# Gate and up projections in pairs of 64-row TensorE tiles, in a fused attention and gated-MLP kernel

## The chip, the cores and the metric

The kernel is one program on one core of a Trainium2 chip. A core has TensorE (PE, matrix products, with its weight loads shown apart as PEld), VectorE (DVE), ScalarE (ACT), GpSimd (POOL) and SyncE (SP, which issues most DMAs). The metric is the device time of the program in microseconds (us); lower is better. The three timed runs shown of the kernel before took 615.78, 615.84 and 615.91 us, median 615.84. The profiled execution took 615.51 us; its span, from the first to the last instruction of the program, is 613.8 us, so 1.7 us lie around the span. The granted TensorE clock was 1.00 over the whole span.

## The reference, cut to what matters

```
xn  = layernorm(x)                         # x: 2048 x 576, no gain or bias
qkv = xn @ wqkv                            # 32 heads of 18
s   = q @ k.T * 18**-0.5                   # query i sees keys i-255 .. i
o   = softmax(s) @ v
h   = silu(xn @ w1) * (xn @ w3)            # 4608 wide: gate w1, up w3
out = x + o @ wo + h @ w2
```

All operands are bf16. Both branches start from the same normalised `xn`, and both end in one sum.

## The kernel before

**Chunks and stages.** The 2048 rows are worked in four chunks of 512 (`c` = 0 to 3). Each chunk has two stages. Stage 1 makes gate, up and `h` for 36 units `u` of 128 hidden columns, and between the units the attention scores, their exps and the products with V. Stage 2 multiplies `h` by `w2` and the attention output by `wo` into four PSUM banks, one for each block of 128 rows, in two passes of 288 columns; beside it the Q, K and V of the next chunk are projected. A prologue normalises chunk 0 and projects its Q, K and V.

**Order.** All engines' work is written out by hand with `add(engine, ...)` in one order. Each engine runs its own instructions in that order, and semaphore waits come from the buffers that an instruction reads and writes. So an instruction that waits holds up all that stands behind it on its engine.

**A unit.** The contraction is 576 deep, which is four blocks of 128 and a rest of 64. `unit_full` (L551, matmuls L556) does the four whole blocks for up and for gate: eight matmuls of 128 x 512, over all 128 rows of the array. `unit_rest` (L561, L567) does the rest in tiles of 32 rows: two for up and two for gate, on two of the array's four row groups. If the unit has an attention step, `window_scores` (L572) puts that step's scores (L460) on the other two row groups. A head is 18 deep and sits in a group of 32 rows. Units without a step are worked in pairs (`window_pair`, L584): both units' rests share the four row groups. There are 120 step units and 12 such pairs.

**A step.** A step is one block of 128 keys for four heads, `g` being the group of heads and `s` the step's number (1 to 3 in chunk 0, else 0 to 3). Its scores are 384 columns a head, one PSUM bank for each head. In steps 0 and 3 a head's columns come from two matmuls. `exps` (L473) runs twice for two heads each, and `masks` (L485) makes four triangle cuts on POOL. Two units after the last step of a group, `pv` (L504) multiplies by V in tiles of 32 array columns, DVE copies the sums to `uT` (L513), `heads_back` (L520) transposes them with four 128 x 128 matmuls, and `heads_out` (L527, L529) divides and stores.

**h.** `us = up * 0.5` (DVE, L593), `th = tanh(gate / 2)` (ACT, L599), `gs = (th + 1) * gate` (DVE, L605), `h = gs * us` (DVE, L608).

**The next chunk's input.** In stage 1 DVE also normalises the next chunk's four blocks of rows: statistics L320 to L322, apply L334 (four instructions, since the 64-row rest is stored four times in two orders for the 32-row tiles). PE transposes a block with six matmuls (L343) and DVE copies it out (L347).

**PSUM.** Four banks go round as a ring for gate, up, `pv` and the transposes; the other four hold the scores in stage 1 and the sums of stage 2.

**Weights.** `load_w13` (L284) brings 512 columns of `w3` and of `w1` at a time into three buffers, and `load_wr` (L296) the 64-row rests apart. `repack` (L413) moves Q and K from `stage` into the layout of the scores by DMA: on SP in chunk 0, on ACT later.

The two lines on which the order inside a step unit rests:

```
unit_rest(c, u, 0); heads 0 and 1; first part of heads 2 and 3
unit_rest(c, u, 1); what is left of heads 2 and 3
```

Of the kernel before, what the change touches and what calls it, by code (L numbers as in the profile page):

```python
# [5 lines left out]
dt = mybir.dt  # L6
# [7 lines left out]
class _Op:  # L14
    __slots__ = ("eng", "fn", "deps", "pos", "sig", "dma", "cnt", "snap", "waits")

    def __init__(self, eng, fn, deps, dma):
        self.eng = eng
        self.fn = fn
        self.deps = deps  # L20
        self.dma = dma
        self.pos = 0
        self.sig = False
        self.cnt = 0
        self.snap = None
        self.waits = ()

# [16 lines left out]
class _Prog:  # L44
# [13 lines left out]
    def add(self, eng, fn, r=(), w=(), j=(), dma=None):  # L58
# [11 lines left out]
        op = _Op(eng, fn, deps, dma)  # L70
# [17 lines left out]
    def resolve(self):  # L88
        know = {e: {} for e in ENGS}
        for op in self.ops:  # L90
            kn = know[op.eng]
            need = {}
            for d in op.deps:
                if d.dma is not None:
                    s, v = ("d", d.dma), d.cnt
                else:
                    if d.eng == op.eng and (d.eng == "pe" or d.eng == "sp"):
                        continue
                    s, v = d.eng, d.pos
# [63 lines left out]
def bass_parallel_sum__sliding_block__glu_gated_swiglu__prompt_kernel(  # L163
# [32 lines left out]
    with ExitStack() as es:  # L196
# [4 lines left out]
        NXP, NOF, NPT, NW13, NW2 = 7, 4, 14, 3, 4  # L201
        ident = sb("ident", [128, 128])
        xp = [sb(f"xp{i}", [128, D]) for i in range(NXP)]
        xn = [sb(f"xn{i}", [128, 768]) for i in range(2)]
# [5 lines left out]
        xnT = sb("xnT", [128, 2, 6, CH])  # L210
        wa = sb("wa", [128, 5, 3 * D])
        wo = sb("wo", [128, 5, D])
        w1 = [sb(f"w1_{i}", [128, 4, 512]) for i in range(NW13)]
        w3 = [sb(f"w3_{i}", [128, 4, 512]) for i in range(NW13)]
        wr = sb("wr", [128, 2, F // 2])
# [3 lines left out]
        qk = sb("qk", [128, 3, G, CH])  # L219
        va = sb("va", [128, 2 * TB, G, 4 * VW])  # L220
        pt = sb("pt", [128, NPT, 2, 384])
        NST = 9 * CH // 768
        pt_more = stage[:, :, :].rearrange("p t c -> p (t c)").rearrange("p (n h q) -> p n h q", h=2, q=384)
# [7 lines left out]
        def st_keys(*tiles):  # L231
            return [("sh", 2 * t + n) for t in tiles for n in range(2)]
# [6 lines left out]
        us = [sb(f"us{i}", [128, CH]) for i in range(2)]  # L239
# [4 lines left out]
        RB = es.enter_context(nc.psum_tensor("rb", [128, 4, 512], dt.float32))  # L244
        SBK = es.enter_context(nc.psum_tensor("sbk", [128, 4, 512], dt.float32))
# [9 lines left out]
        def half_bank(b):  # L255
            return RB[:, b, :].bitcast(dt.bfloat16)

# [18 lines left out]
        def load_w13():  # L276
# [6 lines left out]
            for n, (dst, src) in enumerate(((w3, B_w3), (w1, B_w1))):  # L283
                add("sp", lambda e, dst=dst, src=src: e.dma_start(  # L284
                    dst[s][:], src[0:512, c0:c0 + 512].rearrange("(kd p) f -> p kd f", p=128)),
                    dma=f"w13_{s}", **{"j" if n else "w": [("w13", s)]})

        WR_CUTS = (0, 4, 10, F // 256)

        def load_wr(n):  # L290

            n0, n1 = WR_CUTS[n:n + 2]
            for q in range(4):
                src = (B_w3, B_w1)[q % 2][512:576, :].rearrange("(ab p) (n u f) -> p ab n u f", p=32, u=2, f=128)
                for ab in range(2):
                    add("sp", lambda e, q=q, ab=ab, src=src: e.dma_start(  # L296
                        wr[32 * q:32 * q + 32, ab, n0 * 128:n1 * 128].rearrange("p (n f) -> p n f", f=128),
                        src[:, ab, n0:n1, q // 2, :]),
                        dma=f"wr{n}", **{"j" if q or ab else "w": [("wr", n)]})

        def wr_key(u):
            return ("wr", max(n for n in range(3) if WR_CUTS[n] <= u // 2))

# [14 lines left out]
        def ln_stats(t, s):  # L318
            i = t % 2
            add("dve", lambda e: e.bn_stats(stats[i][:, 0, :], xp[s][:, 0:HD]), r=[("xp", s)], w=[("stats", i)])  # L320
# [7 lines left out]
        def ln_apply(t, s):  # L328
            i = t % 2
            tail = xn[i][:, 512:768].rearrange("p (m a r d) -> p m a r d", m=2, r=2, d=32)  # L330
            xtail = xp[s][:, 512:576].rearrange("p (a d) -> p a d", d=32).unsqueeze(2).to_broadcast([128, 2, 2, 32])
            moves = ((xn[i][:, 0:512], xp[s][:, 0:512]), (tail[:, 0], xtail), (tail[:, 1, 0], xtail[:, 1]), (tail[:, 1, 1], xtail[:, 0]))
            for n, (dst, src) in enumerate(moves):
                add("dve", lambda e, dst=dst, src=src: e.tensor_scalar(  # L334
                    dst, src, mv[i][:, 0:1], rstd[i][:, 0:1], op0=ALU.subtract, op1=ALU.mult),
                    r=[("xp", s), ("mv", i), ("rstd", i)], **{"j" if n else "w": [("xn", i)]})

        def xn_trans(t, bank, key, evac):
            i = t % 2
            c, tt = divmod(t, TB)  # L340
            bv = bank.rearrange("p (k f) -> p k f", f=128)
            for kd in range(6):
                add("pe", lambda e, kd=kd: e.transpose(bv[:, kd, :], xn[i][:, kd * 128:(kd + 1) * 128], ident[:]),  # L343
                    r=[("xn", i), "ident"], **{"w" if kd == 0 else "j": [key]})
            dst = xnT[:, c % 2, :, tt * 128:(tt + 1) * 128]
            if evac == "dve":
                add("dve", lambda e: e.tensor_copy(dst, bv[:, 0:6, :]), r=[key], w=[("xnT", c % 2, tt)])  # L347
            else:
                add("act", lambda e: e.activation(dst, bv[:, 0:6, :], ACT.Copy), r=[key], w=[("xnT", c % 2, tt)])
# [5 lines left out]
        def qk_tile(c, i):  # L355
            b = ring()
            for kd in range(5):
                add("pe", lambda e, kd=kd: e.matmul(  # L358
                    RB[:, b, :], wa[:, kd, i * 128:(i + 1) * 128], xnT[:, c % 2, kd, :],
                    start=(kd == 0), stop=(kd == 4)),  # L360
                    r=["wqk", "wz"] + xk(c), **{"w" if kd == 0 else "j": [("rb", b)]})
            add("dve", lambda e: e.tensor_copy(stage[:, i, :], RB[:, b, :]), r=[("rb", b)], w=st_keys(i))  # L362

        def v_half(c, tt, half, evac):
# [3 lines left out]
            for kd in range(5):  # L368
                add("pe", lambda e, kd=kd: e.matmul(  # L369
                    RB[:, b, 0:HD], xnT[:, c % 2, kd, tt * 128:(tt + 1) * 128], wa[:, kd, c0:c0 + HD],  # L370
                    start=(kd == 0), stop=(kd == 4)),
                    r=["wv", "wz", ("xnT", c % 2, tt)], **{"w" if kd == 0 else "j": [("rb", b)]})
            vv = va[:, slot, :, :].rearrange("p g (hh c) -> p (g hh) c", c=VW)
            dst = vv[:, 16 * half:16 * half + 16, 0:Dh]
            src = RB[:, b, 0:HD].rearrange("p (h d) -> p h d", d=Dh)
            kw = {"w" if half == 0 else "j": [("va", slot)]}
            if evac == "act":
                add("act", lambda e: e.activation(dst, src, ACT.Copy), r=[("rb", b)], **kw)
            else:
                add("dve", lambda e: e.tensor_copy(dst, src), r=[("rb", b)], **kw)  # L380
# [16 lines left out]
        def repack(c, g, eng):  # L397
# [4 lines left out]
            for hh in range(4):  # L402
                b = 1 + c % 2
                for tq, tk, rq, rk, o, n in pieces(Dh * (4 * g + hh)):
                    p0 = 64 * (g % 2) + 32 * (hh % 2) + o
                    gi = 2 * (g // 2) + hh // 2
                    if tq != tk:
                        moves = [(qk[p0:p0 + n, 0:b + 1:b, gi, :], stage[rq:rq + n, tq:tk + 1:tk - tq, :])]
                    else:
                        moves = [(qk[p0:p0 + n, 0, gi, :], stage[rq:rq + n, tq, :]),  # L410
                                 (qk[p0:p0 + n, b, gi, :], stage[rk:rk + n, tk, :])]
# [41 lines left out]
        def score_mms(c, g, s, h):  # L453

            r0 = 64 * (g % 2) + 32 * (h % 2)
            gi = 2 * (g // 2) + h // 2
            for n, (kb, qb, nq, col) in enumerate(parts(c, s)):
                kc, kt = divmod(kb, TB)
                qo = (qb - c * TB) * 128
                add("pe", lambda e, kc=kc, kt=kt, qo=qo, nq=nq, col=col: e.matmul(  # L460
                    SBK[:, h, col:col + 128 * nq],
                    qk[r0:r0 + Dh, 1 + kc % 2, gi, kt * 128:(kt + 1) * 128],
# [386 lines left out]
```

## Time and profile before

| what | value |
|---|---|
| median of the timed runs | 615.84 us |
| profiled execution / its span | 615.51 / 613.8 us |
| busy share PE, DVE, ACT, POOL | 97%, 64%, 43%, 36% |
| prologue | 0 to 25.53 us |
| chunk 0: stage 1, stage 2 | 94.04, 57.34 us |
| chunk 1: stage 1, stage 2 | 92.46, 57.49 us |
| chunk 2: stage 1, stage 2 | 92.47, 57.50 us |
| chunk 3: stage 1, stage 2 | 91.07, 45.89 us |
| DMA | 75.42 MB, mean 123 GB/s |

A stage 1 is counted from its first weight load of L556 to the first of L640, a stage 2 from there to the next stage 1 or the end. The profile names an instruction group by line, engine and tiles. A matmul's duration in the profile (0.38 us for 128 x 512) contains the way through the array; what a following matmul must wait for is the distance between two starts, which is 0.2157 us for matmuls of 128 x 512 one behind the other. Starts are given here to the nanosecond where the trace has them.

### The profile page before, as it was taken

The numbers are of one execution on the slowest core, as the hardware profiler recorded it, in microseconds if no ns is written. First come the engines' busy times: TensorE is split into PE (matmuls) and PEld (weight loads), VectorE is DVE, ScalarE is ACT, GpSimd is POOL, SyncE is SP. The second block draws the span as 40 slices with busy tenths as digits, with TensorE's granted clock in tenths as the row PEclk, the third lists the DMA queues.
The fourth block names the chain that finished last, engine by engine and source line by source line (L and its number), as shares of the span: only waits on it lengthen the run. The fifth ranks groups of instructions, "written<-read, shape, count | busy, mean of one in ns | idle before, by whom it ended". The sixth has DMA issues, their size and how long they took to land.

```text
span 613.8 us, 12327 instructions
## 1 busy us (share of the span) xinstructions
PE 592.5 (97%) x5025; PEld 319.8 (52%) x5092; DVE 392.0 (64%) x762; ACT 262.1 (43%) x397; POOL 220.8 (36%) x521
## 2 busy tenths in 40 slices
PE   5999989999999999999999999999999999999998
PEld 3433333467764444456775444445677443443776
DVE  5579799833138889973405898896340678888311
ACT  4165555500018777730003877771000587777000
POOL 3045545400007666630001766761000376676000
DMA  8555645344544233344453434253445324230352
GB/s 242 155 155 147 182 157 174 116 116 123 139 118 145 82 110 109 118 147 106 114 151 97 137 90 137 70 176 109 110 123 159 104 72 136 69 109 1 97 138 76
DMA packets 100012, 75.42 MB, mean 123 GB/s; under 512 B 11124, under 2 KB 99956, under 8 KB 99956
## 3 DMA queue, kind: packets, MB, share of 16 engines
q1 hardware_dynamic: 95417, 71.09, 40.0%
q10 hardware_dynamic: 4539, 3.54, 2.1%
q8 instruction: 40, 0.66, 0.5%
q14 instruction: 16, 0.13, 0.1%
HBM read 67.53 MB, written 2.36 MB: 114 GB/s over the span
## 4 chain that ended last, share of the span: by engine, by line
PE 93%; DVE 4%; issue 1%; DMA 1%; SPq 0%
PE rb L556 40%; PE sbk L640 23%; PE rb L567 7%; PE rb L358 6%; PE rb L504 4%; PE rb L369 3%; PE sbk L646 3%; PE sbk L460 3%; PE rb L520 2%; DMA wa<-in_A_wqkv_dram 1%; PE rb L343 1%; DVE gs L605 1%; DVE uT L513 1%; DVE us L593 1%; DVE xn L334 1%
## 5 line engine op out<-in xcount | busy, mean ns | idle before, releaser
L556 PE MATMUL rb<-xnT,w 128*128 128x512 bf16 x1095 | 262.3, 380 | 7.9 <-issue 3.0
L485 POOL TENSOR_SCALAR_AFFINE_SELECT pt<-pt 128x256 bf16<-128x256 bf16 x360 | 154.3, 456 | 225.7 <-ACT pt L473 221.3
L599 ACT ACTIVATE th<-rb 128x512 bf16<-128x512 f32 x144 | 85.3, 592 | 213.3 <-PE rb L567 197.8
L473 ACT ACTIVATE pt<-sbk 128x768 bf16<-128x768 f32 x180 | 146.5, 814 | 65.3 <-PE sbk L460 65.3
L556 PEld LDWEIGHTS rb<-xnT,w 128*128 128x128 bf16 x1152 | 102.2, 98 | 135.3 <-issue 25.4
L640 PE MATMUL sbk<-w,hT 128*128 128x288 bf16 x1152 | 157.9, 286 | 0.0
L640 PEld LDWEIGHTS sbk<-w,hT 128*128 128x128 bf16 x1152 | 111.0, 98 | 33.2 <-issue 1.3
L593 DVE TENSOR_SCALAR us<-rb 128x512 bf16<-128x512 f32 x144 | 99.2, 689 | 26.7 <-PE rb L567 22.7
L605 DVE SCALAR_TENSOR_TENSOR gs<-th,rb 128x512 bf16<-128x512 bf16 x144 | 97.7, 678 | 20.5 <-ACT th L599 20.2
L485 POOL TENSOR_SCALAR_AFFINE_SELECT stage<-stage 128x256 bf16<-128x256 bf16 x120 | 52.4, 463 | 87.3 <-ACT stage L473 86.0
L567 PE MATMUL rb<-xnT,wr 32*128 32x512 bf16 x576 | 80.7, 379 | 0.1
L608 DVE TENSOR_TENSOR hT<-gs,us 128x512 bf16<-128x512 bf16 x144 | 64.9, 451 | 5.0
L653 DVE TENSOR_TENSOR ofin<-sbk,xp 128x288 bf16<-128x288 f32 x32 | 14.6, 456 | 73.1 <-PE sbk L646 73.0
L460 PE MATMUL sbk<-qk 18*128 18x384 bf16 (+2 forms) x704 | 59.9, 274 | 0.0
L473 ACT ACTIVATE stage<-sbk 128x768 bf16<-128x768 f32 x60 | 48.8, 814 | 18.0 <-PE sbk L460 18.0
L362 DVE CAST stage<-rb 128x512 bf16<-128x512 f32 x36 | 24.9, 692 | 48.8 <-PE rb L358 48.8
L567 PEld LDWEIGHTS rb<-xnT,wr 32*128 32x128 bf16 x576 | 20.0, 91 | 56.4 <-issue 55.9
L358 PE MATMUL rb<-xnT,wa 128*128 128x512 bf16 x170 | 41.3, 379 | 0.5
L358 PEld LDWEIGHTS rb<-xnT,wa 128*128 128x128 bf16 x180 | 17.6, 98 | 16.0
L646 PE MATMUL sbk<-wo,oT 128*128 128x288 bf16 x160 | 25.8, 286 | 0.0
L369 PE MATMUL rb<-wa,xnT 128*128 128x288 bf16 x160 | 25.2, 296 | 0.1
L513 DVE CAST uT<-rb 128x512 bf16<-128x512 f32 x32 | 22.1, 690 | 5.0 <-PE rb L504 3.3
(42 smaller groups left out, 260.6 us busy)
## 6 DMA issues: line engine op xcount, KB each, us to landing
w<-in_B_w_dram SPq DMA_DIRECT2D x72, 512.0 KB, 4.9
w<-in_B_w_dram SPq DMA_DIRECT2D x72, 288.0 KB, 3.2
xp<-in_A_x_dram SPq DMA_DIRECT2D x32, 144.0 KB, 4.7
qk<-stage ACTq DMA_DIRECT2D x75, 36.0 KB
out_dram<-ofin SPq DMA_DIRECT2D x32, 72.0 KB, 1.6
wa<-in_A_wqkv_dram SPq DMA_DIRECT2D x2, 512.0 KB, 5.9
qk<-stage SPq DMA_DIRECT2D x25, 36.0 KB
wa<-in_A_wqkv_dram SPq DMA_DIRECT2D x1, 576.0 KB, 4.2
```

The source lines that it names most:

```text
L358: add("pe", lambda e, kd=kd: e.matmul(RB[:, b, :], wa[:, kd, i * 128:(i + 1) * 128], xnT[:, c % 2, kd, :], start=(kd == 0), stop=(kd == 4) ...
L460: add("pe", lambda e, kc=kc, kt=kt, qo=qo, nq=nq, col=col: e.matmul(SBK[:, h, col:col + 128 * nq], qk[r0:r0 + Dh, 1 + kc % 2, gi, kt * 128 ...
L473: add("act", lambda e: e.activation(pt_slot(sl), SBK[:, 2 * p:2 * p + 2, 0:384], ACT.Exp, scale=scale), r=[("sb", 2 * p), ("sb", 2 * p + 1 ...
L485: add("pool", lambda e, vb=vb, edge=edge: e.affine_select(out=vb, in_=vb, compare_op=ALU.is_ge, fill=0.0, base=-1 if edge else 0, pattern= ...
L556: add("pe", lambda e, kd=kd, b=b, ws=ws: e.matmul(RB[:, b, :], ws[sl][:, kd, fl * 128:(fl + 1) * 128], xnT[:, c % 2, kd, :], start=(first ...
L567: add("pe", lambda e, b=b, r0=r0, n0=n0, start=start: e.matmul(RB[:, b, :], wr[r0:r0 + 32, ab, n0:n0 + 128], xnT[r0:r0 + 32, c % 2, 4 + (a ...
L593: add("dve", lambda e: e.tensor_scalar(us[i][:], RB[:, bu, :], 0.5, None, op0=ALU.mult), r=[("rb", bu)], w=[("us", i)])
L599: add("act", lambda e: e.activation(th[i][:], RB[:, bg, :], ACT.Tanh, scale=0.5), r=[("rb", bg)], w=[("th", i)])
L605: add("dve", lambda e: e.scalar_tensor_tensor(out=gs[i][:], in0=th[i][:], scalar=1.0, in1=RB[:, bg, :], op0=ALU.add, op1=ALU.mult), r=[("t ...
L608: add("dve", lambda e: e.tensor_tensor(hT[:, u, :], gs[i][:], us[i][:], ALU.mult), r=[("gs", i), ("us", i)], w=[("h", u)])
L640: add("pe", lambda e: e.matmul(bank, hT[:, f, tt * 128:(tt + 1) * 128], w2[sl][:, k, :], start=(f == 0), stop=False), r=[("h", f), ("w2", ...
L646: add("pe", lambda e: e.matmul(bank, oT[:, tt, k, :], wo[:, k, d0:d0 + HD], start=False, stop=(k == 4)), r=[("oT", tt), "wo", "wz"], j=key)
```

## The change

PSUM becomes one tensor `PS` of eight banks. Units take banks 0 and 1 or 2 and 3 in turn; bank 4 is `SPARE`, used by `pv`, the transposed heads and the next chunk's transposes in stage 1; a step's scores lie in banks 5 to 7 without gaps. In stage 2 banks 4 to 7 hold the sums, and 0 to 3 are the ring.

- `w13` holds `w3` in partitions 0 to 63 and `w1` in partitions 64 to 127, nine blocks of 64 rows each. `unit_pairs` (L599) runs a unit as nine pairs: up on the array's lower 64 rows, gate on its upper 64 rows. For four of the nine pairs it reads `xnS`, a copy of `xnT` with its two halves exchanged, which two DMAs on ACT's queue make once for each chunk (`xn_swap`). The loads of the rests (`load_wr`) are gone.
- A head's scores are 64 deep: two heads share 64 rows, and Q is stored twice, with zeros in place of the other head. POOL clears these buffers in the prologue.
- `unit_break` (L462, L532) writes a step's scores for both halves of the array, in an order in which the halves never write one bank at the same time, with a wait of PE for itself before the last part. The transposes of `uT` and `xn` are split into two halves of 64 rows (4 or 5 matmuls of 64 columns each), beside the scores.
- One exp for 1536 columns (L477), and two masks of 512 columns (L489).
- `h` is `gs = (th + 1) * gate`, `h = gs * 0.5 * up` with `up` read from PSUM (L613, L616).
- `xn` is 640 wide, written by two instructions (L318); five transposes a block; `heads_out` and `xn_evac` (L328) come behind `unit_h` on DVE. First statistics one unit earlier than the rest.
- Steps start at unit 4g+1 in chunk 0 and 4g+3 later; `pv` (L507) comes behind `unit_break`; what falls past the last unit moves into stage 2.

```
-        xn = [sb(f"xn{i}", [128, 768]) for i in range(2)]
+        xn = [sb(f"xn{i}", [128, 640]) for i in range(2)]
+        xnS = sb("xnS", [128, 4, CH])
+        w13 = [sb(f"w13_{i}", [128, 9, 512]) for i in range(NW13)]
-        qk = sb("qk", [128, 3, G, CH])
+        qk = sb("qk", [128, 4, G, CH])
-        pt = sb("pt", [128, NPT, 2, 384])
+        pt = sb("pt", [128, NPT, 4, 384])
+        SPARE, ACC = 4, (4, 5, 6, 7)
+        SC = PS[:, 5:8, :].rearrange("p b c -> p (b c)")
...
+            for n, src in enumerate((B_w3, B_w1)):
+                add("sp", lambda e, n=n, src=src: e.dma_start(
+                    w13[s][64 * n:64 * n + 64, :, :], src[:, c0:c0 + 512].rearrange("(kd p) f -> p kd f", p=64)),
...
+        def xn_swap(c):
+            for n in range(2):
+                p, q = 64 * n, 64 - 64 * n
+                add("act", lambda e, p=p, q=q: e.dma_start(
+                    xnS[p:p + 64, :, :], xnT[q:q + 64, c % 2, 0:4, :]),
+                    r=xk(c), dma="xnS", **{"j" if n else "w": ["xnS"]})
...
+        def score_mm(c, g, s, h, blk0, nblk, first, after=()):
+            r0 = 64 * (h // 2)
...
+                done = add("pe", lambda e, kc=kc, kt=kt, qo=qo, n=n, col=col: e.matmul(
+                    SC[:, col:col + n],
+                    qk[r0:r0 + 64, 2 + kc % 2, g, kt * 128:(kt + 1) * 128],
+                    qk[r0:r0 + 64, h % 2, g, qo:qo + n],
+                    start=True, stop=True, tile_position=(r0, 0)),
...
+        def half_trans(r, b, nblk, src, key, after=()):
+            bv = half_bank(b).rearrange("p (k f) -> p k f", f=128)
+            r0 = 64 * r
+            for k in range(nblk):
+                yield add("pe", lambda e, k=k: e.transpose(
+                    bv[:, k, r0:r0 + 64], src[r0:r0 + 64, k * 128:(k + 1) * 128], ident[r0:r0 + 64, r0:r0 + 64],
+                    tile_position=(r0, 0)),
...
+        def unit_break(c, step, trans):
...
+            if step is None:
+                last = None
+                for last in low:
+                    pass
+                if trans is not None:
+                    for _ in half_trans(1, SPARE, nblk, src, key, (last,)):
+                        pass
+                return
+            g, s = step
+            d01 = score_mm(c, g, s, 2, 0, 2, True)
+            for last in low:
+                pass
+            score_mm(c, g, s, 3, 0, 3, True)
+            score_mm(c, g, s, 0, 0, 3, True)
+            score_mm(c, g, s, 2, 2, 1, False)
+            score_mm(c, g, s, 1, 0, 1, False)
+            if trans is not None:
+                up = half_trans(1, SPARE, nblk, src, key, (last,))
+                next(up)
+            score_mm(c, g, s, 1, 1, 2, False, (d01,))
+            for _ in up:
+                pass
...
+        def unit_pairs(c, u):
+            b0 = 2 * (u % 2)
+            for n in range(9):
+                for r in range(2):
+                    r0 = 64 * r
+                    k = 8 if n == 8 else (2 * n + r if n < 4 else 2 * (n - 4) + 1 - r)
+                    src = xnT[r0:r0 + 64, c % 2, k // 2, :] if n in (0, 1, 2, 3, 8) else xnS[r0:r0 + 64, n - 4, :]
+                    add("pe", lambda e, n=n, r0=r0, r=r, k=k, src=src: e.matmul(
+                        PS[:, b0 + r, :], w13[sl][r0:r0 + 64, k, fl * 128:(fl + 1) * 128], src,
+                        start=(n == 0), stop=(n == 8), tile_position=(r0, 0)),
...
-            add("dve", lambda e: e.tensor_scalar(us[i][:], RB[:, bu, :], 0.5, None, op0=ALU.mult),
-            add("dve", lambda e: e.tensor_tensor(hT[:, u, :], gs[i][:], us[i][:], ALU.mult),
+            add("dve", lambda e: e.scalar_tensor_tensor(
+                out=hT[:, u, :], in0=gs[i][:], scalar=0.5, in1=PS[:, bu, :], op0=ALU.mult, op1=ALU.mult),
...
+            at_unit = {(4 * g + 1 if c == 0 else 4 * g + 3) + n: (g, s)
+                       for g in range(G) for n, s in enumerate(steps_of(c))}
+            pv_unit = {last[g] + 2: g for g in range(G)}
+            fin_unit = {u + 2: g for u, g in pv_unit.items()}
+                xt_unit = {u: i for i, u in enumerate((14, 20, 26, 32) if c == 0 else (9, 17, 25, 33))}
...
+                unit_pairs(c, u)
...
+                unit_break(c, step, trans)
                 unit_tanh(u)
                 if step is not None:
+                    exps(c, *step)
+                unit_h(u)
                 if u in fin_unit:
                     heads_out(fin_unit[u])
+                elif u in xt_unit:
+                    xn_evac((c + 1) * TB + xt_unit[u], SPARE, "dve")
+                if u in pv_unit:
+                    pv(c, pv_unit[u], SPARE)
+                    pv_out(pv_unit[u])
```

## The prediction, on record before the changed kernel was run

> **What bounds the kernel now.** I read the page's busy shares first, then its chain, then the waits of PE, then a table by stage.
>
> ```profile
> span 613.8 us, 12327 instructions
> ...
> PE 592.5 (97%) x5025; PEld 319.8 (52%) x5092; DVE 392.0 (64%) x762; ACT 262.1 (43%) x397; POOL 220.8 (36%) x521
> ...
> PE 93%; DVE 4%; issue 1%; DMA 1%; SPq 0%
> ...
> L599 ACT ACTIVATE th<-rb 128x512 bf16<-128x512 f32 x144 | 85.3, 592 | 213.3 <-PE rb L567 197.8
> L473 ACT ACTIVATE pt<-sbk 128x768 bf16<-128x768 f32 x180 | 146.5, 814 | 65.3 <-PE sbk L460 65.3
> ...
> L593 DVE TENSOR_SCALAR us<-rb 128x512 bf16<-128x512 f32 x144 | 99.2, 689 | 26.7 <-PE rb L567 22.7
> L605 DVE SCALAR_TENSOR_TENSOR gs<-th,rb 128x512 bf16<-128x512 bf16 x144 | 97.7, 678 | 20.5 <-ACT th L599 20.2
> ...
> L608 DVE TENSOR_TENSOR hT<-gs,us 128x512 bf16<-128x512 bf16 x144 | 64.9, 451 | 5.0
> ```
>
> PE is on the chain for 93% of the span and the other engines have room. So only PE's order of starts counts, and others only where PE waits for them:
>
> ```profile
> PE rb L504 <- DVE gs L605: 1.6, 2, 0.8
> PE rb L556 <- DVE gs L605: 1.4, 2, 0.7
> PE rb L556 <- DVE us L593: 1.1, 7, 0.2
> PE rb L556 <- DVE rden L527: 0.9, 2, 0.6
> PE rb L520 <- DVE uT L513: 0.8, 4, 0.2
> ```
>
> The columns are total us, times, longest. These waits lie nearly all in chunk 0, where stage 1 takes 94.04 us for fewer steps than the 92.46 of chunk 1. What one unit costs is read from PE's timeline (start, busy us):
>
> ```profile
> 342.39 0.39 PE L567 MATMUL rb<-xnT,wr 32*128 32x512 bf16 x2
> 342.39 0.50 PE L460 MATMUL sbk<-qk 18*128 18x384 bf16 x4
> 342.61 0.38 PE L567 MATMUL rb<-xnT,wr 32*128 32x512 bf16 x2
> 342.92 1.90 PE L556 MATMUL rb<-xnT,w 128*128 128x512 bf16 x8
> 344.75 0.39 PE L567 MATMUL rb<-xnT,wr 32*128 32x512 bf16 x2
> ```
>
> Four row groups start within 10 ns of each other: tiles do run side by side. From 342.39 to 344.75, a step unit takes 2.369. Inside, whole-array matmuls start 0.2157 apart, and a row group's second matmul of 512 columns 0.226 after its first. The last of L556 starts 0.308 before the first of L567, the last of L567 0.302 before the next L556: about 0.09 more than its columns, each time the tiling changes. So a unit pays about 0.2 us for two changes. That is what the change can win; it pays with a ninth pair (0.216) and a longer score window.
>
> **The sum, part by part** (after minus before, us over the whole run).
>
> 1. **Step units, +6.5.** Nine pairs at 0.2157 are 1.941. Is 0.2157 right for 64-row tiles? In the step windows in tiles, later starts of one row group are 0.056 (128 columns) and 0.109 (256) apart, as in the whole array; only the first after a change is 0.010 longer. I take 0.2157, with 0.226 as upper end (+13.3 for 1296 pairs) and nothing lower. The scores: I assume that a matmul doesn't start before the one ahead of it in program order, even on a free half, because all starts in the trace come in program order. Then in steps 1 and 2 the chain is 256, 384, 128, 256 columns: 0.109 + 0.163 + 0.056 + 0.109 = 0.44. In step 0 the split parts make it 128+128, 128, 128, 256, 128, 256: 0.50; in step 3 256, 256, 256, 128, 128, 128, 128: 0.55. So units of 2.38 (twice), 2.44, 2.49 against 2.369: +0.22 for a group of four steps, 24 groups, +5.3; chunk 0 (steps 1 to 3) 8 x 0.15 = +1.2. If the halves ran on their own, the last part would still wait for the first one's end (0.107 + 0.161 + about 0.05 to signal), and each window would be 0.436: +1.0 in all. The trace has no case that tells; I take the order, both ends stay.
>
>  The Trainium skill, "TensorE: Matmul & The Clock Gate", Part 3, says matmuls issue strictly first in, first out, starts and ends alike; by it the sum stays +6.5.
>
> 2. **Units without a step, -2.6.** A pair is 1.833 + 0.543 + 1.726 = 4.10, twelve times; two units after are 3.88.
>
> 3. **Waits for DVE, -5.6.** The rows above, by distances of starts: 8 pair windows 1.3, chunk 0 4.3. DVE loses L593 (689) and its last operation grows from 451 to about 678 (the row with the same operands, L605): 0.46 less per unit. If half of the waits stayed, +2.8.
>
> 4. **Heads' transposes, -5.8.** L520 took 0.184 and lengthened the next start by 0.040, 32 times 7.2. After, 28 lie beside the scores of step 3: a half is 4 matmuls of 64 columns, 0.029 each if columns set it (half of 0.053 plus 0.0025), 0.117 beside 0.109 of scores: +0.01. One in chunk 0 stands in a unit without step (0.42), three stay in stage 2. The pitch's upper end is the row L520 itself, 0.056 for 128 columns: +5.9 with part 5. I take 0.029, as the 128-column pitch equals its columns.
>
>  Against this speaks the skill's same page, section on LDWEIGHTS: a weight load takes its columns at 1.2 GHz, 107 ns for 128, whatever the rows. The row L520 denies it, four loads and matmuls 0.056 apart. By the rule each half would be 0.43, some +16 with part 5.
>
> 5. **Input transposes, -2.6.** Twelve times 0.295 + 0.040 = 4.0 becomes 10 x 0.043 beside scores and 2 x 0.48 without step.
>
> 6. **Prologue, -0.2.** One transpose fewer in each of four blocks. POOL's clears start at 10.0; by the 0.82 of its 864-element memset they take 3.9 and 1.9, done at 15.8, before SP's first repack (19.1). That repack is issued by 22.6; the first scores now come at about 29.1 instead of 35.8. The exchanged copy (512 KB) has from 15 to 26; ACT issues it, and behind it stand two V copies with 2 us to spare. SP loses 24 loads of 0.43; its w13 loads use half the partitions, but are needed 19 us later (landing now 4.9). If any of it is late, it is 1 to 3 us once.
>
> 7. **pv, +2.8.** It is the one part of stage 1 in another tiling. Before, it stood at a change that was paid anyway; now it brings its own: 28 x 0.10.
>
> 8. **New waits, +5.8.** SPARE is one bank for three users. (a) Units with an input transpose are followed by one with heads: DVE copies out only behind `h`. From the last pair's end: tanh at 0.19 to 0.79, gs 0.82 to 1.50, h to 2.2, copy (548 for 768 columns, some 0.48 for 640) to 2.61, signal 0.05; the next window begins at 0.48 + 1.94 = 2.42: 0.25, 10 times, +2.5. All later scores and pairs stand behind. (b) In chunk 0 units 20 and 32 follow a head unit, whose division ends at 2.9 against 2.5: +0.8. (c) Stage 2's first matmul writes bank 4: in chunk 0 the last heads are in unit 35, ready at 0.42, free at 2.92: +2.5; later chunks about +0.15, +0.15, +0.4; before's own late starts there (0.7) go.
>
> **What stays hidden.** ACT: tanh 0.48 to the next start, then exp of 1536 columns, 0.814 + 768 x 0.87 ns = 1.48 (slope from 592 and 814): done at 2.15 of 2.38. Cover 0.2; each 0.05 beyond it costs 6 us. POOL: two masks of 512 instead of four of 256 (456): less than before, and `pv` reads them 1.5 us later.
>
> Sum: 6.5 - 2.6 - 5.6 - 5.8 - 2.6 - 0.2 + 2.8 + 5.8 = -1.7. Against the profiled run (615.51, that is 613.8 of span and 1.7 around) it gives 613.8. The median of the timed runs is 0.33 above it: **614.1**.
>
> **Rivals.**
>
> - A, faster: the halves don't hold each other up. Part 1 is +1.0: 608.6. For it: row groups start freely in the windows. Against: no start out of order.
> - B, slower: 64-row pairs keep the first pitch, 0.226, at every pair, since loads of both halves alternate: +13.3, 627.4. It decides from 0.2170 on, 1.7 / 1296 above 0.2157, where the gain is gone. For it: no row group in the trace runs more than a few tile matmuls in a row. Against: 0.056 and 0.109.
> - C, slower: half transposes start 0.056 apart: 620.0.
> - D, slower: PE's wait for itself, or for the exp, adds 0.05 in each of 120 step units: +6, 620.1. For it: the wait is met at about 0.32, just where its part could start.
> - E: up and gate aren't side by side at all: 1296 x 0.2157 more, some 894. The four starts within 10 ns exclude it nearly.
>
> **Chances.** Forecast with its small errors (612 to 618) 0.46, A 0.12, B 0.12, C 0.11, D 0.13, E 0.01, others, evenly to both sides, 0.05. A measurement of this kernel tells some 0.2% (1.2 us) from no change. Of the forecast's 0.46, 0.29 is below 614.6 and 0.05 above 617.1. Faster: 0.29 + 0.12 + 0.02 = 0.43; same 0.12 + 0.01 = 0.13; slower 0.05 + 0.12 + 0.11 + 0.13 + 0.01 + 0.02 = 0.44. The range takes in A's neighbourhood, C and D and leaves out B: 607.5 to 622.5.
>
> **What would show it.** Starts of L599 in one half 0.2157 apart (B: 0.226). Windows from the last pair to the next of 0.44, 0.44, 0.55, 0.50 in turn (A: 0.436 all). Starts of L532 0.029 apart (C). PE waits for L328 ten times 0.25, for L574 at the end of chunk 0 with 2.5; no wait for the exp (D). Stage 1 of chunk 0 about 90 us, of chunk 1 about 93. What makes it wrong most easily is a few ns on each of 1296 pairs.

## The result and the profile after

The changed kernel takes 618.79 us, median of five runs (618.16 to 620.58), against 615.91 us (615.78 to 616.58) of the kernel before in the same comparison: a ratio of 1.005, 95% interval 1.0032 to 1.0068. It is slower by half a per cent. The forecast was 614.1 us with a range of 607.5 to 622.5: the time lies in the range, the sign is wrong. The profiled execution took 618.35 us, 2.84 more than that of before.

The page of the kernel after, with the lines that answer to those of before:

```profile
span 616.6 us, 14288 instructions
...
PE 597.2 (97%) x6290; PEld 376.2 (61%) x6300; DVE 338.5 (55%) x587; ACT 255.6 (41%) x277; POOL 168.3 (27%) x284
...
PEclk9899999999999999999999999999999999999999
...
PE 92%; DVE 6%; ACT 1%; issue 1%; POOL 0%
...
L613 DVE SCALAR_TENSOR_TENSOR gs<-th,ps 128x512 bf16<-128x512 bf16 x144 | 99.0, 687 | 104.0 <-ACT th L607 103.7
...
L477 ACT ACTIVATE pt<-ps 128x1536 bf16<-128x1536 f32 x87 | 125.7, 1445 | 0.9
...
L616 DVE SCALAR_TENSOR_TENSOR hT<-gs,ps 128x512 bf16<-128x512 bf16 x144 | 98.9, 687 | 4.9
```

DVE has 53.5 us less to do and is 6% of the chain instead of 4%: a busy share says nothing about who sets the end. The second slice of PEclk, an 8, is new. The granted clock does not tell all of it: before's profile has no clock record, for which its views put 1.00, and after's record begins only at 14.14 us. PE's starts fill the gap. In before's timeline ten matmuls of one form take 2.58 us at the start of the program and 1.39 us three us later:

```profile
9.04 2.58 PE L369 MATMUL rb<-wa,xnT 128*128 128x288 bf16 x10
12.02 1.39 PE L369 MATMUL rb<-wa,xnT 128*128 128x288 bf16 x10
```

They start 0.240 apart first and 0.122 later. So each of these kernels starts at half pace, until 11.9 us in before and 14.1 us in after. By stage, the windows view of after (columns: length, busy time of PE, PEld, DVE, ACT and POOL, each with its count, granted clock, DMA share, GB/s; these are the prologue, stages 1 and 2 of chunk 0, and stage 1 of chunk 1):

```profile
0.00:32.01 32.01, 21.16 (x104) 11.65 (x105) 20.11 (x32) 7.39 (x13) 12.04 (x20) 0.95 0.82 179
32.01:124.63 92.62, 88.81 (x1048) 50.07 (x1048) 68.01 (x120) 53.91 (x60) 32.55 (x56) 1.00 0.81 162
124.63:180.66 56.03, 55.84 (x430) 41.45 (x433) 14.97 (x28) 0.00 (x0) 0.00 (x0) 1.00 0.57 145
180.66:272.99 92.33, 91.93 (x1153) 51.25 (x1153) 67.35 (x116) 64.43 (x68) 41.66 (x72) 1.00 0.62 122
```

| | before | after | measured | predicted |
|---|---|---|---|---|
| prologue | 25.53 | 32.01 | +6.48 | -0.2 |
| chunk 0, stages 1 + 2 | 151.38 | 148.65 | -2.73 | not given apart |
| all behind the prologue | 588.3 | 584.6 | -3.7 | -1.5 |

The steady part of the kernel gained more than predicted. Stage 1 of chunk 0 takes 92.62, or 90.2 without the wait of 2.4 at its end (forecast: about 90), stage 1 of chunk 1 92.33 (about 93). The loss is in the prologue, where the prediction had put nearly nothing. DVE's and POOL's timelines of after there (start, length, and in brackets the idle time ahead):

```profile
9.28 7.55 DVE L318 TENSOR_SCALAR xn<-xp,mv,rstd 128x576 bf16<-128x576 bf16 x2 [0.56 <-POOL rstd L312]
```

```profile
9.19 3.51 POOL L721 MEMSET qk<- 128x4096 f32 x1
12.64 1.80 POOL L707 MEMSET qk<- 128x2048 f32 x1
14.38 0.33 POOL L723 MEMSET wo<- 64x288 f32 x1
14.66 1.80 POOL L707 MEMSET qk<- 128x2048 f32 x1
```

L318 normalises a block of rows in two instructions. The wide one of the last block takes 7.35 us; those of the three blocks ahead of it took 0.38 to 0.43. It begins 0.1 us behind POOL's first clear and ends 0.2 us behind the last. PE waits for it, and then runs at half clock, as PE's timeline and the windows view of the same stretch show:

```profile
11.69 2.60 PE L365 MATMUL ps<-wa,xnT 128*128 128x288 bf16 x10
16.89 0.45 PE L336 MATMUL ps<-ident,xn 128*128 128x128 bf16 x5 [2.60 <-DVE xn L318]
17.18 4.28 PE L365 MATMUL ps<-wa,xnT 128*128 128x288 bf16 x20
```

```profile
17.55:20.97 3.42, 3.42 (x17) 2.19 (x15) 0.00 (x0) 1.62 (x4) 0.00 (x0) 0.50 1.14 207
```

PE is busy all through this stretch. 3.42 us at 0.50 do the work of 1.71, so it costs 1.71. (L365 ahead of it, ten matmuls in 2.60 us, is still in the slow start.) The waits of PE in after:

```profile
PE ps L336 <- DVE xn L318: 9.2, 3, 5.8
PE ps L649 <- DVE oall L572: 3.4, 4, 2.4
PE ps L532 <- DVE oall L572: 1.2, 2, 0.6
PE ps L599 <- DVE stage L358: 0.9, 1, 0.9
PE ps L365 <- DMA wa<-in_A_wqkv_dram: 0.8, 1, 0.8
PE ps L599 <- DVE hT L616: 0.6, 3, 0.2
```

Of before's waits for `gs`, `us`, `rden` and `uT`, 5.8 us together, 0.6 behind `h` are left. Two lines behind `oall`, the heads' division, are new, and so is the first pair's wait for the last copy into `stage`.

### The profile page after: what moved, and what is told of

Its sections match the earlier page's. It is cut to its first block, busy times and chain, and to the rows that moved or that the text cites. A ratio compares the mean times of both kernels' runs of the same rounds, so it can differ in the third digit from the quotient of the medians.

```text
span 616.6 us, 14288 instructions
## 1 busy us (share of the span) xinstructions
PE 597.2 (97%) x6290; PEld 376.2 (61%) x6300; DVE 338.5 (55%) x587; ACT 255.6 (41%) x277; POOL 168.3 (27%) x284
## 4 chain that ended last, share of the span: by engine, by line
PE 92%; DVE 6%; ACT 1%; issue 1%; POOL 0%
PE ps L599 43%; PE ps L649 23%; PE ps L462 8%; PE ps L354 6%; PE ps L507 4%; PE ps L655 3%; PE ps L365 3%; DVE xn L318 2%; PE ps L532 1%; DVE hT L616 1%; DVE gs L613 1%; ACT th L607 1%; PE ps L581 1%; DVE oall L572 0%; POOL rstd L312 0%
## 5 line engine op out<-in xcount | busy, mean ns | idle before, releaser
L607 ACT ACTIVATE th<-ps 128x512 bf16<-128x512 f32 x144 | 86.0, 597 | 300.2 <-PE ps L599 295.5
L599 PE MATMUL ps<-xnT,w 64*128 64x512 bf16 x1440 | 208.7, 377 | 1.5 <-DVE stage L358 0.9
L649 PE MATMUL ps<-w,hT 128*128 128x288 bf16 x1152 | 157.3, 286 | 3.4 <-DVE oall L572 3.4
L488 POOL TENSOR_SCALAR_AFFINE_SELECT pt<-pt 128x512 bf16<-128x512 bf16 x174 | 106.7, 640 | 191.4 <-ACT pt L477 191.4
L613 DVE SCALAR_TENSOR_TENSOR gs<-th,ps 128x512 bf16<-128x512 bf16 x144 | 99.0, 687 | 104.0 <-ACT th L607 103.7
L599 PE MATMUL ps<-xnS,w 64*128 64x512 bf16 x1152 | 151.6, 376 | 0.0
L649 PEld LDWEIGHTS ps<-w,hT 128*128 128x128 bf16 x1152 | 112.0, 98 | 37.9 <-issue 5.4
L477 ACT ACTIVATE pt<-ps 128x1536 bf16<-128x1536 f32 x87 | 125.7, 1445 | 0.9
L599 PEld LDWEIGHTS ps<-xnT,w 64*128 64x128 bf16 x1440 | 74.8, 94 | 54.4 <-issue 6.7
L599 PEld LDWEIGHTS ps<-xnS,w 64*128 64x128 bf16 x1152 | 69.0, 94 | 55.4
L616 DVE SCALAR_TENSOR_TENSOR hT<-gs,ps 128x512 bf16<-128x512 bf16 x144 | 98.9, 687 | 4.9
L462 PE MATMUL ps<-qk 64*128 64x128 bf16 (+2 forms) x888 | 79.2, 251 | 0.0
L462 PEld LDWEIGHTS ps<-qk 64*128 64x128 bf16 x888 | 51.8, 94 | 32.9 <-ACT pt L477 1.4
L477 ACT ACTIVATE stage<-ps 128x1536 bf16<-128x1536 f32 x33 | 47.7, 1445 | 0.3
L365 PE MATMUL ps<-wa,xnT 128*128 128x288 bf16 x160 | 28.1, 320 | 0.8 <-DMA wa<-in_A_wqkv_dram 0.8
```

The source lines that it names most:

```text
L365: add("pe", lambda e, kd=kd: e.matmul(PS[:, b, 0:HD], xnT[:, c % 2, kd, tt * 128:(tt + 1) * 128], wa[:, kd, c0:c0 + HD], start=(kd == 0), ...
L462: done = add("pe", lambda e, kc=kc, kt=kt, qo=qo, n=n, col=col: e.matmul(SC[:, col:col + n], qk[r0:r0 + 64, 2 + kc % 2, g, kt * 128:(kt + ...
L477: add("act", lambda e: e.activation(pt_slot(sl).rearrange("p h q -> p (h q)"), SC, ACT.Exp, scale=scale), r=[("ps", b) for b in (5, 6, 7)] ...
L488: add("pool", lambda e, vb=vb, edge=edge: e.affine_select(out=vb, in_=vb, compare_op=ALU.is_ge, fill=0.0, base=-1 if edge else 0, pattern= ...
L599: add("pe", lambda e, n=n, r0=r0, r=r, k=k, src=src: e.matmul(PS[:, b0 + r, :], w13[sl][r0:r0 + 64, k, fl * 128:(fl + 1) * 128], src, star ...
L607: add("act", lambda e: e.activation(th[i][:], PS[:, bg, :], ACT.Tanh, scale=0.5), r=[("ps", bg)], w=[("th", i)])
```

## The experiments

The theory: DVE's apply is held off by POOL's clears, with which it shares no data, and this costs the prologue most of its 6 us. Its rivals for the prologue: the clears delay something else (a queue, a repack), or the size of the apply alone makes it long.

**The clears later.** In the changed kernel the first clear waits for the last normalised block, so that all of POOL's clears lie behind DVE's apply:

```
-  add("pool", lambda e: e.memset(qk[:, 0:2, ...], 0.0), w=[("q", g) for g in range(G)])
+  add("pool", lambda e: e.memset(qk[:, 0:2, ...], 0.0), r=[("xn", 1)], w=[("q", g) for g in range(G)])
```

> The changed kernel with one more read on the first POOL clear of qk, so that all three clears start when DVE has written the last normalised block (about 10 us). Theory P (a DVE instruction that meets a POOL memset stands until POOL is done: L318 took 7.35 us, from 9.28 to 16.63, while POOL cleared from 9.19 to 16.46): that L318 takes about 0.43, the first pair starts near 25.5 instead of 32.0, and the time is 618.8 - 6.5 = 612.3. Rival Q (the w13 loads into half the partitions, the first of which is issued at 9.30, hold DVE up): nothing changes, 618.8. Rival R (another wait in the prologue is late next, first of all the projection of Q and K, which needs POOL's clear of wo behind the clears): about 25.5 to 28, 612 to 615.

614.27 us (12 runs, 612.41 to 616.66), ratio 0.9978 (0.9963 to 0.9994): 4.5 us below the changed kernel, and now slightly below the kernel before. DVE's timeline:

```profile
9.27 0.64 DVE L318 TENSOR_SCALAR xn<-xp,mv,rstd 128x576 bf16<-128x576 bf16 x2 [0.55 <-POOL rstd L312]
```

Both instructions together take 0.64 us instead of 7.55, so their size is not what makes them long. The clears end 0.8 us later than before the edit and nothing waits for them. The runs fall into two groups by granted clock: six at 1.00 over the span took 612.41 to 613.57, six at 0.997 took 614.98 to 616.66. The profiled one is of the second group, and its windows view shows where, at the start of stage 2 of chunk 0, beginning 0.4 us before the end of PE's wait of 2.4 us for the heads of unit 35:

```profile
119.00:122.70 3.70, 3.07 (x14) 1.92 (x15) 0.46 (x1) 0.00 (x0) 0.00 (x0) 0.54 0.96 222
```

PE works 3.0 us at half clock there, which costs 1.5; the means of the two groups, 613.0 and 615.9, are 2.8 apart, so this does not explain all of the difference.

**The kernel before with the clears.** The same loads on POOL, cleared into a buffer that is not in use yet:

```
+  add("pool", lambda e: e.memset(hT[:, 0:16, :].bitcast(dt.float32), 0.0), w=[...])
+  add("pool", lambda e: e.memset(hT[:, 16:24, :].bitcast(dt.float32), 0.0), w=[...])
   add("pool", ... memset of wo ...)
+  add("pool", lambda e: e.memset(hT[:, 24:32, :].bitcast(dt.float32), 0.0), w=[...])
```

> The kernel before with three POOL memsets of the same sizes (4096, 2048 and 2048 words of hT, which is free then) where the changed kernel has its clears. Output unchanged. Theory P: the last apply (L334) stands about 7 us, the first L556 comes near 32, the time is 615.9 + 6.5 = 622.4. Rival Q (the new loads): 615.9.

622.08 us (621.91 to 622.53), ratio 1.0103 (1.009 to 1.0116). The clears, with nothing else of the change, cost 6.3 us. The timeline of DVE and PE's waits in this kernel:

```profile
8.86 9.11 DVE L334 TENSOR_SCALAR xn<-xp,mv,rstd 128x512 bf16<-128x512 bf16 x8
```

```profile
PE sbk L343 <- DVE xn L334: 12.4, 3, 6.2
```

In the kernel before this wait was 7.3 us in all; 5.1 us are added, and the granted clock is 0.50 for 3.41 us behind the wait, which costs about 1.7 more. No queue and no repack of the change is needed for it.

**The clears in pieces.** In the changed kernel, 32 clears of 256 words in place of three of 4096 and 2048:

```
-  e.memset(qk[:, 0:2, :, :].bitcast(dt.float32), 0.0)
+  for n in range(2 * G): e.memset(qk[:, n // G, n % G, :].bitcast(dt.float32), 0.0)
   ... # the two clears of 2048 likewise
```

> The changed kernel with its POOL clears in 32 memsets of 256 words each... that is one per head group and slot, at the old place. If POOL holds DVE off only for the length of one instruction, L318 slips in after the first piece (below 0.5 us) and the time is 612 to 613.5. If DVE stands as long as POOL has work, 618.8 as the changed kernel. Under rival Q 618.8 too.

621.09 us (seven runs, 615.33 to 621.84), ratio 1.0063 (1.0034 to 1.0091). DVE's and POOL's timelines:

```profile
9.27 8.54 DVE L318 TENSOR_SCALAR xn<-xp,mv,rstd 128x576 bf16<-128x576 bf16 x2 [0.55 <-POOL rstd L312]
```

```profile
9.19 4.10 POOL L723 MEMSET qk<- 128x256 f32 x16
13.23 2.08 POOL L708 MEMSET qk<- 128x256 f32 x8
15.26 0.33 POOL L726 MEMSET wo<- 64x288 f32 x1
15.54 2.23 POOL L708 MEMSET qk<- 128x256 f32 x8
```

The wide instruction takes 8.25 us, through all of these clears but the last, so here DVE does not get in between two clears that start 0.25 us apart. Two of the seven runs took 615.3 and 615.6; perhaps it did in them, but they have no trace. Nor does it always stand as long as POOL has the next one ready. Beside two masks, one straight behind the other, the same pair of instructions in the timelines of after takes 1.38 us:

```profile
200.43 1.38 DVE L318 TENSOR_SCALAR xn<-xp,mv,rstd 128x576 bf16<-128x576 bf16 x2
200.48 1.29 POOL L488 TENSOR_SCALAR_AFFINE_SELECT pt<-pt 128x512 bf16<-128x512 bf16 x2 [0.68 <-ACT pt L477]
```

The wide one ends 0.16 us behind the first mask (at 201.28, against 201.12), and the second mask takes 0.70 instead of 0.64: there the two engines take turns. What decides between the two cases stays open.

**The apply in another form.** The clears at their old place, and the last block of chunk 0 normalised by the same formula as `scalar_tensor_tensor` with `rstd` broadcast along the row:

```
+  if t == TB - 1:
+      e.scalar_tensor_tensor(out=xn[i][...], in0=xp[s][:, c0:c1], scalar=mv[i][:, 0:1],
+          in1=rstd[i][:, 0:1].to_broadcast([128, c1 - c0]), op0=ALU.subtract, op1=ALU.mult)
```

> The changed kernel with its POOL clears at the old place; only the last block's apply in the prologue is written as a scalar_tensor_tensor with the reciprocal deviation broadcast as second operand, so that DVE takes it in another mode. Theory P1 (POOL holds off only the DVE instructions that run in the fast mode of L318): the apply takes 0.6 to 0.8, the first pair starts near 26.5, 612 to 614. P2 (any DVE instruction from SBUF to SBUF stands while POOL clears): L318's place again 7 us, 618.8.

614.06 us (613.24 to 616.08), ratio 0.9976 (0.9965 to 0.9987). DVE, POOL and PE in this kernel (its lines are numbered 6 higher than in after: L342 is the transposes, L371 and L360 the projections):

```profile
9.27 1.01 DVE L319 SCALAR_TENSOR_TENSOR xn<-xp,mv,rstd 128x576 bf16<-128x576 bf16 x2 [0.56 <-POOL rstd L312]
```

```profile
9.18 3.51 POOL L727 MEMSET qk<- 128x4096 f32 x1
```

```profile
13.06 0.44 PE L342 MATMUL ps<-ident,xn 128*128 128x128 bf16 x5
13.34 2.61 PE L371 MATMUL ps<-wa,xnT 128*128 128x288 bf16 x20
16.01 9.66 PE L360 MATMUL ps<-xnT,wa 128*128 128x512 bf16 x44
26.54 0.82 PE L605 MATMUL ps<-xnT,w 64*128 64x512 bf16 x6 [0.87 <-DVE stage L364]
```

The apply runs beside the very clear that held it off before: the wide one takes 0.82 us. So it is the fast one-input form that waits for POOL's clear, not DVE as such. (The two-input form was run beside a clear alone, which only writes, and not beside a mask, which also reads.) The Trainium skill, "SBUF — State Buffer", section "SBUF: two separate sides", states this: DVE and GpSimd share one pair of ports as an exclusive lock, taken by an operation of GpSimd or by a DVE operation in a two-port fast mode, and the loser stands still. The runs agree, with 7.35 us against 0.82. In one thing they differ: the page has the lock held for one instruction, while DVE stood through a row of them.

This gives the prologue's 6.48 us, term by term. In after PE waits 2.60 for the held apply and loses 1.71 to the half clock behind it, together 4.31 of the 32.01. The 27.70 that are left are 1.19 more than this kernel's 26.51, and these are not the clears': in after the slow start lasts until 14.14, here until 12.21, and 1.93 us more at half pace cost 0.97; the weights `wa` let L365 begin at 8.78 against 8.57, the other 0.2. Where the slow start ends differs from one execution to the next: in the four profiles of kernels with this prologue and late clears it ends between 11.36 and 14.28. The rest, 0.98, is still there at 26.51 against 25.53, and beside it stands a wait of 0.87 that the kernel before does not have, of the first pair for a copy out of `stage`'s last bank.

**That wait.** The best kernel below, with the ring of banks moved on by two ahead of the first projections of Q and K and again behind them, so that unit 0 finds its banks free:

```
+  for _ in range(2): ring()
   for _ in qk_atoms(0, issue_first):
       pass
+  for _ in range(2): ring()
```

> The kernel with the late clears and the early copies, and in the prologue the ring of banks moved on by two ahead of the projections of Q and K and again behind them, so that the last of these projections lies in bank 2 and no longer in bank 0, which unit 0 needs first. If the 0.9 us that the first pair waits for the last copy into stage is what is left of the prologue's loss (26.31 against 25.53 us in the kernel before): the wait goes, the prologue is about 25.5, the span about 0.8 shorter than 604.7, the median near 606.3. If another thing holds the first pair as well (weights, the loads' order, the exchanged copy), the wait only takes another name and the median stays at 607.1. Nothing behind the prologue may change.

607.56 us (607.16 to 607.89) against 607.06 of the kernel it starts from: nothing gained, as the rival expected. The wait for `stage` is gone, and PE's timeline shows another one ahead:

```profile
17.95 9.66 PE L354 MATMUL ps<-xnT,wa 128*128 128x512 bf16 x44 [0.82 <-ACT va L374]
27.54 1.04 PE L599 MATMUL ps<-xnT,w 64*128 64x512 bf16 x8
```

V's and then Q's and K's projections go through one ring of banks, and the wait moves to where the ring meets ACT's copies of V. In this execution the weights `wa` came some 0.6 us later than in that of the best kernel, and the slow start lasted to about 14 us instead of 11.4, so the last 1 us of the prologue is not settled.

**Upper half first.** For step 1 of the prediction: in the kernel with late clears, two score matmul groups of the two halves change places in program order. If matmuls started only in program order, as I had assumed, the windows would change; if each half runs on its own, nothing would.

```
+  score_mm(c, g, s, 2, 2, 1, False)
   score_mm(c, g, s, 0, 0, 3, True)
-  score_mm(c, g, s, 2, 2, 1, False)
```

> e1 with all upper-half scores ahead of the lower-half ones in program order (no bank is shared by the halves at any time, nothing else changed). If matmuls start only in program order (as the prediction assumed), the lower half starts behind the upper's last one and each of 120 windows grows by about 0.15: +18, 630. If the halves run on their own (rival A): as e1 within 1 us, 612.

613.61 us (ten runs, 612.93 to 617.88), ratio 0.9978 (0.9961 to 0.9995); runs at clock 1.00 took 612.93 to 613.71, beside 612.41 to 613.57. By distances of `tanh` starts, a step unit is 2.396 in both. The order inside a window is without effect. After's own timeline shows why:

```profile
345.28 0.59 PE L462 MATMUL ps<-qk 64*128 64x256 bf16 x8
345.66 0.39 PE L599 MATMUL ps<-xnT,w 64*128 64x512 bf16 x1
345.72 0.22 PE L462 MATMUL ps<-qk 64*128 64x128 bf16 x1
345.77 1.02 PE L599 MATMUL ps<-xnT,w 64*128 64x512 bf16 x7
```

The next unit's first pair (L599, 345.66) starts on the lower half 0.06 us before the last score (L462, 345.72) on the upper, which stands ahead of it in program order. The Trainium skill, "TensorE: Matmul & The Clock Gate", Part 3, has matmuls start and end strictly in program order; between two tiles of 64 rows this trace differs, and the measurement decides.

**Copies ahead of `h`.** For the waits of part 8: in the kernel with late clears, DVE copies the input transposes out ahead of `h` in their units, and divides the heads ahead of `h` in chunk 0's units that somebody waits for:

```
-  unit_h(u)
+  early = u in xt_unit or u in fin_unit and (u >= 33 or u + 1 in xt_unit)
+  if not early:
+      unit_h(u)
   ...heads_out, xn_evac...
+  if early:
+      unit_h(u)
```

> e1 with DVE's copy of the input transposes (L328) ahead of gs and h of its unit, and the heads' division (L570, L572) ahead of them in the units from 33 on and in those followed by an input transpose. By the waits measured in the changed kernel: L532 behind L328 (10 times, 2.5 us of units 2.654 instead of 2.405) goes, L532 behind L572 (1.2) goes, L649 behind L572 (3.4, longest 2.4) falls by about 1.5 at the end of chunk 0 and by some 0.5 in the later ones: together 5 to 6 below e1, 607 to 608. Theory C (a PE pause of 2 us or more is followed by one stretch of 3.41 us at a granted clock of 0.5): with the pause at the end of chunk 0 below 1 us, no run shows the dip there and the runs of this kernel spread less than e1's 612.4 to 616.7. Rival (gs and h, now later, hold up the unit after next): units grow by some 0.2 and the gain is half.

607.06 us (606.43 to 607.6), ratio **0.986** (0.9847 to 0.9874): this version beats both kernels, by 8.8 us the one before. All runs have clock 1.00. PE's waits of this kernel:

```profile
PE ps L336 <- DVE xn L318: 6.6, 2, 5.8
PE ps L649 <- DVE oall L572: 0.9, 1, 0.9
PE ps L599 <- DVE stage L358: 0.9, 1, 0.9
PE ps L599 <- DVE hT L616: 0.6, 3, 0.2
```

Units with heads behind an input transpose take 2.439 instead of 2.654 (ten times), units 20 and 32 of chunk 0 2.71 instead of 3.23, and the waits ahead of stage 2 (L649) fall from 3.4 to 0.9, the one in chunk 0 from 2.4 to 0.9: 2.15 + 1.04 + 2.5 = 5.7. The runs differ by 6.0 where both have clock 1.00 over the span.

**Only the copies of the input.** The same with `early = u in xt_unit`:

> The kernel with the late clears, and of the early copies only those in the units with an input transpose: DVE copies the transposes out ahead of h there, while the division of the heads stays behind h. By the sum of part 8: the waits of L532 behind L328 go, ten times 0.25, and the 0.6 us twice in chunk 0 and the 2.4 us ahead of stage 2 of chunk 0 stay. So about 2.5 us less than the kernel with the late clears alone (612.4 to 613.6 where the clock is full): 610 to 611, and with a stretch at half clock behind the 2.4 us wait 1.7 more. If the whole gain of the early copies came from the chunk 0 waits, it is 612.4 to 613.6.

612.24 us (seven runs, 610.75 to 615.1), ratio 0.9949 (0.9931 to 0.9967); those at clock 1.00 took 610.75, 611.96 and 612.16, a little above the expected 610 to 611. Nine of the ten units take 2.44, one has a pause of PE of 1.0 us that no wait explains. The waits that this edit leaves alone are still in the view:

```profile
PE ps L649 <- DVE oall L572: 3.8, 4, 2.4
PE ps L532 <- DVE oall L572: 1.2, 2, 0.6
```

Four of the seven runs show 0.997 again. The kernels with the pause of 2.4 us ahead of stage 2 have that clock in some of their runs (six of twelve, four of ten, three of eight, four of seven), those without it in none of eight. Over a span this doesn't tell where: in the profile of the kernel with the upper half first the stretch lies elsewhere.

**Two operations for `h` alone.** For part 3: the kernel before without L593, and `h = gs * 0.5 * up` from PSUM.

```
-  e.tensor_tensor(hT[:, u, :], gs[i][:], us[i][:], ALU.mult)
+  e.scalar_tensor_tensor(out=hT[:, u, :], in0=gs[i][:], scalar=0.5, in1=RB[:, bu, :], ...)
-  unit_scale(u)
```

> The kernel before with one part of the change alone: h in two DVE operations (no L593; the second one reads up from PSUM). Part 3 of the prediction: DVE has 0.46 us less per unit, the waits of PE for DVE in chunk 0 (5.6 by distances of starts) go, 610.3. Rival: up's bank is now held until h, 1.4 us longer, and the ring of four banks gives new waits of PE in the units with pv, heads or input transposes; then 613 to 620.

739.57 us (735.8 to 740.86), ratio 1.1998 (1.1969 to 1.2026). Both theories missed widely. PE's waits:

```profile
PE rb L556 <- DVE hT L608: 96.1, 91, 2.5
```

In before's ring of four banks `us = up * 0.5` set up's bank free early. Without it, the bank is held until `h`, and the ring stands. So in before's ring the shorter `h` can't be had by itself; in the changed kernel the next unit has the other pair of banks. What part 3 gained can't be told from the rest by undoing it.

## Why the prediction was wrong, point by point

**The step that failed is part 6, the prologue:** "POOL's clears start at 10.0 ... done at 15.8, before SP's first repack", -0.2. 3.9 and 1.9 count two clears where there are three (3.51, 1.80 and 1.80, with that of `wo` from 9.19 to 16.46); but nothing waited for their end, so that was not the error. Their place was judged only by who reads their output. The cost lay with an engine that shares no data with them. It measured +6.5: 2.60 of waiting for the held apply, 1.71 for the clock behind it, 1.2 for a slow start that lasted longer and for later weights, 1.0 at the first pair's wait for a bank. Without the hold the kernel takes 614.1 to 614.3, which is the forecast; that is luck, since part 1 was wrong by 5.5 the other way, as the rest of this list shows. A row of before could have warned me. This is the view of L334 there:

```profile
L334 DVE TENSOR_SCALAR xn<-xp,mv,rstd x64: 287/334/632, 5.1 to 408.5; 128x64 bf16<-128x64 bf16 x32, 128x512 bf16<-128x512 bf16 x16, 128x128 bf16<-128x128 bf16 x16
```

One form of 512 columns has durations from 359 to 632 ns. Each one above 490 lay beside masks of POOL for its whole length, and the shorter ones beside POOL's work for 0.32 at most. Such a spread within one form is a reason to ask what the form shares with whom. I had read means.

- **Part 1, step units, +6.5: wrong, measured +1.0.** "A matmul doesn't start before the one ahead of it in program order, even on a free half" fell. Units are 2.395 (steps 0 to 2) and 2.327 (step 3), a mean window of 0.436 as rival A had it. (How a group's time is split between steps, heads and pv is partly a choice: the first group of chunk 1, with neither heads nor pv in its units, has 2.400, 2.325, 2.328 and 2.332.) The 0.2157 of a pair held, so B is out (a unit without step is 1.942 for nine pairs); E is out too. PE's wait for itself is met, as D feared, but its signal takes about 0.06, near the 0.05 that A's window contains.
- **Part 2, units without step, -2.6: right** (1.942 against the 1.941 assumed).
- **Part 3, waits for DVE, -5.6: right in the view** (5.8 us of waits became 0.6), with DVE's second operation 687 against 678. Its cause was named too narrowly: in before's ring the banks do not allow it.
- **Parts 4 and 5, transposes.** The pitch of 0.029 held (C is out). A unit with heads costs 0.078 more, not 0.01, 28 times: +1.9. A unit with an input transpose costs 0.069, not 0.043.
- **Part 7, pv, +2.8: right** (0.859 on top of a step unit against 0.864).
- **Part 8, new waits, +5.8: right in place and nearly in size.** (a) 0.25 ten times as predicted, (c) 2.4 against 2.5; (b) 1.29 a unit instead of 0.90, +0.8. The price of a wait in PE's clock was missing: where the 2.4 us pause is followed by the half clock, it costs 1.5 more by the profile with late clears.
- **The chances.** Faster at 0.43 and slower at 0.44 were even; the case that came true was in none of the rivals. "If any of it is late, it is 1 to 3 us once" was too small a price, and it had no chance of its own.

From the predicted -1.7: -5.5 (part 1) + 6.7 (part 6) + 1.9 + 0.3 + 0.8 (parts 4, 5, 8b) = +2.5, against +2.84 measured. Pauses of PE that no wait explains lengthen units 16 and 19 of chunk 2 by 0.28 and 0.17 in after's profile, which covers the 0.3 that is left. The first and the second correction nearly cancel.

## What to carry to other kernels

When work is added to an engine, ask not only who reads its result but who runs beside it and shares something with the engine: here POOL clears of 7.3 us, for whose end nothing waited, stopped a DVE operation of 0.4 us on the critical path. Look at the spread of one form's durations, not the mean: a form that takes 359 to 632 ns is worth the question what runs beside it. And price a PE pause of over 2 us with what the clock may do after it. When two profiles' first microseconds are compared, look first where the slow start ends in each. A few waits of DVE removed by order alone were worth 6.0 us here, more than the reshaping of the matmuls with the clears out of the way (2.8, by the runs at clock 1.00).

## What the runs showed of the hardware

- **DVE's one-input form stands while POOL works.** L318 at 576 columns took 0.42 us alone, 0.85 beside a mask of 0.64, 7.35 beside the three large clears. The same block by the two-input form took 0.82 beside the clear.
- **A row of short clears can hold DVE as long as large ones:** 32 clears 0.25 us apart held it for 8.25 us. Between two masks it got in, and the second mask took 0.70 instead of 0.64.
- **The halves of the array run on their own** where tiles of 64 rows are used; a later matmul of one half (345.66) starts before an earlier one of the other (345.72).
- **PE starts at half pace.** In every one of these kernels the first matmuls of 288 columns start 0.240 apart and later ones 0.122; the change came between 11.3 and 14.3 us into the span.
- **Pauses of PE of 2.1 to 2.6 us can bring the half clock back.** In the profiles, the kernel with two operations for `h` left out, four of eight such pauses were followed, or met before their end, by a stretch of 3.4 us at 0.50: the one in the prologue of after (all five of whose runs have a clock below 1.00 over the span), the one ahead of stage 2 in two kernels with late clears, and a pause of 2.1 us that no wait explains in the kernel with the upper half first. The pauses of 5.1 us (before with clears) and 4.7 us (clears in pieces) were, too. What tells the four from the other four stays open.
